# Heads of 22 float64 weight pieces: two ScalarE activations replaced by two GpSimd multiplications

## Chip, cores and metric

One core of a Trainium2 chip runs the whole program in one launch. The metric is the device time of that core in microseconds (us). The engines are TensorE (PE in the profile, its weight loads PEld), VectorE (DVE), ScalarE (ACT), GpSimd (POOL) and SyncE (SP), which issues most of the DMA transfers.

## The reference

Three stages follow one another. Attention with a top-32 mask over 4 x 8 heads gives 2304 token rows of 512. A routing step gives each token to one of 8 experts, greedily by falling logit and with at most 288 tokens each. Each expert is a two-layer network; what it gives goes through one more layer pair, whose weights w_in and w_out are float64.

```
scores = scale * q @ k.T ; keep the 32 largest of a row ; softmax ; x = attn @ v
for idx in argsort(-(x @ w_gate).flatten()):        # routing
    tok, e = idx // E, idx % E
    if assigned[tok] < 0 and counts[e] < cap: assigned[tok] = e; counts[e] += 1
for e in range(E):
    y[mask_e] = maximum(x[mask_e] @ w1[e], 0) @ w2[e]
h = y @ w_in
g = (a0 + a1*h + a2*h*h + a3*h**3) / (1 + |b0|*|h| + |b1|*h*h + 1e-6)
out = g @ w_out                                      # w_in, w_out: float64
```

## The kernel before

**The stages in time.** Attention fills the first 442 us of the profiled execution. The routing search follows up to about 553 us, then the gathers of the first experts' tokens are prepared. From about 568 to 624 us lies a stretch that is called the transition here: PE computes expert 0's two layers while ACT and DVE finish w_in and w_out. From 624 us on PE multiplies by w_in and w_out, expert after expert, to the end.

**The float64 pieces.** TensorE works on float16 here, so each float32 or float64 weight becomes a pair of float16 numbers, high and low. w_in and w_out are cut into 32 pieces of 128 x 512 numbers: pieces 0 to 15 are w_in, 16 to 31 w_out, in blocks of four. `fetch` lets SP load a raw piece into a slot (of `region`, `win`, `wout` or `nraw`; the slot's name stands in the rows). A piece then goes through these steps:

- The heads. They take the top 16 bits of each float64 number (sign, 11 bits of exponent, 4 of fraction) and make of them the top of a float32. For the pieces of `quick` (6 to 19 before) these are two ACT instructions into a `ring` tile, of which there are three: Abs (L373) and Relu (L377). `signed` (L395) puts the sign in, and `mantissa` (L408) the lower bits of the fraction; both are DVE instructions on halves of 256 columns. For the other pieces from 6 on, the heads are three ACT instructions (L383 Sign, L384 Abs, L385 Relu), and DVE does `mantissa` and `apply_sign` (L412) on 512 columns.
- ACT squares the piece and sums (`square`, L306). When a block of four is done, a few small DVE instructions make its scales s_in or s_out (L293 to L298).
- ACT writes the scaled high part (`high`, L436), DVE the low part (`low`, L440). The raw slot is then free, and `fetch` loads the next piece into it.

When all of w_out's scales stand, DVE takes their minimum (ev_m, L1363), PE turns it (L1356), and behind these in PE's order stand the norm (L2061) and the first products with w_in (ph, L1929 to L1931).

**What sets the order.** A planner (class Flow) is given every one of these instructions with its engine, a cost, a rank and what it waits for, and writes each engine's instruction list before the program runs. Each engine carries its list out in order, and an instruction that is not ready holds up all that stand behind it. POOL's list holds, in routing, the updates of the assignment (asel L1690, asg L1711), and in the transition the gathers xe of the experts' token rows (L1906).

The program's functions that the diff touches:

Of the kernel before, what the change touches and what calls it, by code (L numbers as in the profile page):

```python
# [9 lines left out]
BF16 = mybir.dt.bfloat16  # L10
# [174 lines left out]
def kernel(  # L185
# [163 lines left out]
    bias16 = wpool.tile([P, 1], F32, name="bias16")  # L349
    nc.vector.memset(bias16, -896.0 * 2.0**7)  # L350
    QS = int(6)
    QE = int(20)
    ring, ring_of, ring_users = [], {}, []

    def quick(n):
        return QS <= n < QE
# [10 lines left out]
    def heads(n):  # L367
        top = top_of(n)
        if quick(n):
            def size():  # L370
                ring.append(ring.pop(0))
                ring_of[n] = ring[-1]
                nc.scalar.activation(upper_of(n).bitcast(BF16), top.bitcast(BF16), AF.Abs)  # L373

            return [
                ("A", 0.52, size),
                ("A", 0.52, lambda: nc.scalar.activation(  # L377
                    upper_of(n), upper_of(n), AF.Relu, scale=2.0**3, bias=bias16
                )),
            ]  # L380
        top = top.bitcast(BF16)
        return [
            ("A", 0.52, lambda: nc.scalar.activation(sign(n), top, AF.Sign)),  # L383
            ("A", 0.52, lambda: nc.scalar.activation(top, top, AF.Abs)),  # L384
            ("A", 0.61, lambda: nc.scalar.activation(  # L385
                value(n).bitcast(U32), top.bitcast(U16), AF.Relu, scale=2.0**19, bias=bias8
            )),
        ]
# [3 lines left out]

    def signed(n, o):
        up = upper_of(n)[:, o]
        nc.vector.scalar_tensor_tensor(up, top_of(n)[:, o], 0x8000, up, op0=OP.bitwise_and, op1=OP.bitwise_or)  # L395

    def in_parts(cost, fn, deps, rank, late, hv=None):

# [20 lines left out]
    def add_block(i, n0, dst, s, inv, rows, rank, late, after):  # L419

        o = slice(4 * i, 4 * i + 4) if rows else slice(i, i + 1)
        sq = wpool.tile([P, 4], F32, name="nq", bufs=8)
        steps = []
        n2 = sq
        if not rows:
            n2 = wpool.tile([P, 1], F32, name="nq1", bufs=8)
            steps.append(("V", 0.07, lambda: nc.vector.tensor_reduce(n2, sq, axis=AX.X, op=OP.add)))
        steps += [("V", 0.07, f) for f in power_steps(s[:, o], inv[:, o], n2, 410)]

        def part(g):  # L430
            j = 4 * i + g if rows else i
            return j, [d[:, j, :] if rows else d[:, i, g * 512 : (g + 1) * 512] for d in dst]

        def high(g):
            j, (h, l) = part(g)
            nc.scalar.activation(h, value(n0 + g).bitcast(F32), AF.Copy, scale=s[:, j : j + 1])  # L436

        def low(g):
            j, (h, l) = part(g)
            nc.vector.scalar_tensor_tensor(  # L440
                l, value(n0 + g).bitcast(F32), s[:, j : j + 1], h, op0=OP.mult, op1=OP.subtract
            )
            fetch(raw_t.pop(n0 + g))

        norms = []
        for g in range(4):
            n = n0 + g
            t = [arrived[n]]
            if quick(n):
                first = flow.add("A", 0.52, lambda n=n: heads(n)[0][2](), t, rank + 0.5, late)  # L450
                t = flow.add("A", 0.52, lambda n=n: heads(n)[1][2](), [first], rank + 0.5, late)
                t = in_parts(0.6, lambda o, n=n: signed(n, o), [t], rank + 0.4, late)
                t = in_parts(0.6, lambda o, n=n: mantissa(n, o), t, rank + 0.3, late)
                take(first, ring_users, ZR, t)
            else:
                for k in range(3 if n >= 6 else 0):
                    t = [flow.add("A", (0.52, 0.52, 0.61)[k], lambda n=n, k=k: heads(n)[k][2](), t, rank + 0.5, late)]
                if n >= EV:
                    parts = 1 if n >= QE else HV
                    t = in_parts(0.6, lambda o, n=n: mantissa(n, o), t, rank + 0.4, late, parts)  # L460
                    t = in_parts(0.6, lambda o, n=n: apply_sign(n, o), t, rank + 0.3, late, parts)
            norms.append(
                flow.add("A", 0.61, lambda n=n, g=g: square(value(n).bitcast(F32), sq[:, g : g + 1]), t, rank + 0.2, late)
            )
        scaled = flow.chain(steps[:-1], norms, rank, late)
        lows, LOWS = [], after
        last = flow.chain(steps[-1:], [scaled], rank + 0.3, late)
        for g in range(4):
            t = flow.add("A", 0.61, lambda g=g: high(g), [scaled] + (lasts[-1] if lasts else []), rank + LOWS, late)
            t = flow.add("V", 0.66, lambda g=g: low(g), [t], rank + LOWS + 0.1, late)  # L470
            lows.append(t)
        lasts.append(lows)
        return last

    with ExitStack() as actx:
# [862 lines left out]
            for i in range(2):  # L1338
                fetch((arena2[:, i, 1024 * b : 1024 * (b + 1)], 4 * KC + 4 * b - 1, None))
        for i in range(ZR):  # L1340
            ring.append(lpool.tile([P, 512], U32, name=f"ring{i}", bufs=1))
            nc.gpsimd.memset(ring[-1], 0)
        NRAW = 4
        for i in range(NRAW):
            fetch((npool.tile([P, 1024], U32, name=f"nraw{i}", bufs=1), NP, None))

# [1047 lines left out]
```

## Time and profile before

| | before |
|---|---|
| median of three runs | 1222.1 us (1221.91 to 1222.24) |
| profiled execution | 1227.85 us, span 1226.1 us |
| PE busy | 1114.8 us (91%) |
| DVE busy | 1056.6 us (86%) |
| ACT busy | 1021.4 us (83%) |
| POOL busy | 381.4 us (31%), 487 instructions |
| granted TensorE clock, mean | 0.921 |

Shares are means over stages with different limits. The profiled execution is a run of its own beside the three; its span is the time from its first to its last recorded instruction. POOL's busy time lies almost all in attention.

### The profile page before, as it was taken

How to read it: one execution, taken by the hardware profiler on the slowest of the kernel's cores; microseconds unless marked ns; L12 is line 12 of the kernel's file. 1: busy time of each engine (PE TensorE's matmuls, PEld its weight loads, DVE VectorE, ACT ScalarE, POOL GpSimd, SP SyncE). 2: the span in 40 equal slices, each digit the busy share in tenths (PEclk: the TensorE clock that was granted, in tenths of full speed). 3: DMA queues.
4: the chain of work that ended last, by engine and by line, in shares of the span. 5: the costliest groups of instructions: out<-in, count | busy, mean ns of one | idle time of the engine just before them, and what ended most of it. 6: DMA issues, size and time to landing. Idle time of an engine off the chain costs nothing.

```text
span 1226.1 us, 26893 instructions
## 1 busy us (share of the span) xinstructions
PE 1114.8 (91%) x9719; PEld 900.6 (73%) x9719; DVE 1056.6 (86%) x4094; ACT 1021.4 (83%) x1810; POOL 381.4 (31%) x487
## 2 busy tenths in 40 slices
PE   4899999999999986884749999999999999999996
PEld 3688888888888854653536778888888888888784
DVE  6999999988989937886898879898989889897795
ACT  4899999999999847577989978888888788876684
POOL 4788888877778400002010001110101000001010
PEclk9899999999999975555978999999999999999998
DMA  5205202112000307411242222221112221000000
GB/s 125 51 10 162 50 13 51 36 34 51 2 2 1 138 2 285 148 53 58 104 151 76 69 89 89 89 88 70 56 54 89 89 78 68 33 2 20 1 21 20
DMA packets 81105, 80.59 MB, mean 66 GB/s; under 512 B 59968, under 2 KB 59968, under 8 KB 80960
## 3 DMA queue, kind: packets, MB, share of 16 engines
q1 hardware_dynamic: 77888, 69.27, 17.9%
q0 software_dynamic: 3072, 9.48, 2.6%
q8 instruction: 80, 1.31, 0.4%
q14 instruction: 65, 0.53, 0.1%
HBM read 69.25 MB, written 9.47 MB: 64 GB/s over the span
## 4 chain that ended last, share of the span: by engine, by line
PE 27%; issue 15%; ACT 6%; DVE 4%; POOL 1%; DMA 1%; POOLq 0%; DVEq 0%
PE pa L1929 3%; PE pa L1930 3%; PE ph L1929 3%; PE pa L1931 3%; PE ph L1930 3%; PE ph L1931 3%; PE po L1930 3%; PE po L1931 3%; PE po L1929 3%; ACT junk L306 2%; POOL out_dram L2315 1%; ACT w1s L1402 1%; PE pa L2304 0%; ACT wout L383 0%; DVE w2s L1407 0%
## 5 line engine op out<-in xcount | busy, mean ns | idle before, releaser
L785 POOL TENSOR_TENSOR win<-sv,sg 128x576 f32<-128x576 f32 x142 | 179.3, 1284 | 65.2 <-ACT sg L780 49.6
L749 DVE MAX8 cd<-sv 128x8 f32<-128x82 f32 (+1 forms) x1008 | 178.5, 231 | 12.0 <-ACT sv L702 11.9
L1929 PE MATMUL ph<-x,win 128*128 128x288 f16 x512 | 148.2, 289 | 11.2 <-DVE uv L2198 11.2
L883 PE MATMUL po<-vm,pT 128*128 128x65 f32 (+1 forms) x1280 | 151.3, 266 | 0.7 <-DVE x L903 0.4
L1930 PE MATMUL po<-g,wout 128*128 128x288 f16 x512 | 147.6, 288 | 2.2 <-DVE g L1920 2.1
L1929 PE MATMUL po<-g,wout 128*128 128x288 f16 x512 | 147.6, 288 | 0.9 <-ACT g L1919 0.8
L1930 PE MATMUL ph<-x,win 128*128 128x288 f16 x512 | 148.2, 289 | 0.0
L1931 PE MATMUL ph<-x,win 128*128 128x288 f16 x512 | 148.2, 289 | 0.0
L1931 PE MATMUL po<-g,wout 128*128 128x288 f16 x512 | 147.6, 288 | 0.0
L883 PEld LDWEIGHTS po<-vm,pT 128*128 128x128 f32 (+1 forms) x1280 | 139.3, 182 | 3.4 <-PE pt L855 1.1
L851 PE MATMUL pt<-ident,sv 128*128 128x128 f32 x648 | 126.3, 283 | 0.0
L2315 POOL DMA_INDIRECT out_dram<-ob,tok x24 | 25.5, 1063 | 317.5 <-ACT ob L2311 266.7
L855 PE MATMUL pt<-dg,mk 128*128 128x128 bf16 x720 | 120.5, 221 | 1.5 <-POOL mk L842 1.3
L1906 POOL DMA_INDIRECT xe<-xrows,rows_i x24 | 24.6, 1026 | 297.9 <-PE pa L1941 274.8
L780 ACT ACTIVATE sg<-sv,cut_all 128x576 bf16<-128x576 f32 x142 | 109.3, 779 | 4.9 <-DVE cut_all L755 4.9
L2189 ACT ACTIVATE z<-ph,inv 128x288 f32<-128x288 f32 x128 | 64.0, 500 | 59.0 <-PE ph L1931 58.4
L841 ACT ACTIVATE sg<-sv,pn 128x576 bf16<-128x576 f32 x136 | 98.2, 774 | 12.9 <-POOL pn L819 12.9
L692 PE MATMUL s<-region 64*128 64x288 f32 (+1 forms) x640 | 92.7, 438 | 16.2 <-ACT region L663 11.8
L786 DVE MAX8 w<-win 128x8 f32<-128x576 f32 x142 | 105.5, 744 | 0.0
L851 PEld LDWEIGHTS pt<-ident,sv 128*128 128x128 f32 x648 | 92.5, 143 | 16.2 <-issue 3.9
L842 POOL TENSOR_SCALAR mk<-sg 128x576 bf16<-128x576 bf16 x136 | 89.1, 674 | 1.8
L865 ACT ACTIVATE pT<-pt 128x1152 f32<-128x1152 f32 x72 | 81.4, 1131 | 4.8 <-PE pt L855 4.6
(359 smaller groups left out, 3315.7 us busy)
## 6 DMA issues: line engine op xcount, KB each, us to landing
region<-in_moe_w_dram SPq DMA_DIRECT2D x16, 2048.0 KB, 7.9
xrows<-x SPq DMA_DIRECT2D x1, 4644.0 KB
region<-in_q_dram SPq DMA_DIRECT2D x32, 128.0 KB, 2.8
region<-in_k_dram SPq DMA_DIRECT2D x32, 128.0 KB, 2.7
vm<-in_v_dram SPq DMA_DIRECT2D x32, 128.0 KB, 3.1
wout<-in_moe_w_in_dram SPq DMA_DIRECT2D x8, 511.8 KB, 6.8
region<-in_moe_w_out_dram SPq DMA_DIRECT2D x8, 511.8 KB, 3.4
win<-in_moe_w_in_dram SPq DMA_DIRECT2D x6, 511.8 KB, 7.8
```

Source lines behind the costliest of these rows:

```text
L692: nc.tensor.matmul(sc[p0 : p0 + n, 2 * hh + g, 0:w], qT[rows, j, p0 : p0 + n], kT[rows, bb, c : c + w], start=True, stop=True,)
L749: nc.vector.max(cd[:, g, :], sv[:, o : o + n])
L780: nc.scalar.activation(sg, sv_t[u, hh], AF.Sign, bias=cut_all[:, 2 * u + hh, 7:8], scale=-OVER, accum_out=t["sum"][:, c : c + 1],)
L785: nc.gpsimd.tensor_tensor(win, sv_t[u, hh], sg, op=OP.mult)
L786: later.append(lambda c=c, win=win: nc.vector.max(t["w8"][:, c, :], win))
L841: nc.scalar.activation(sg, sv, AF.Sign, bias=t["pn"][:, c : c + 1])
L851: nc.tensor.transpose(dst, pr[:, c * P : (c + 1) * P], ident)
L855: nc.tensor.matmul(dst, mk_buf[u % 2][:, o : o + P], bat[b]["dg"][:, 2 * i + hh, :], start=False, stop=True, skip_group_check=True,)
L883: nc.tensor.matmul(po[p0 : p0 + n, i, hh, :], sb[:, hh * (R + 1) + c, p0 : p0 + n], vm[:, bb, hh, c, :], start=(c == 0), stop=False,)
L1929: nc.tensor.matmul(acc, ah, bh, start=first, stop=False)
L1930: nc.tensor.matmul(acc, ah, bl, start=False, stop=False)
L1931: nc.tensor.matmul(acc, al, bh, start=False, stop=last)
```

## The change

Pieces 6 to 27 are now `quick`. Their heads are two POOL instructions: `narrow` multiplies the top 16 bits, read as bfloat16, by 2^-112 into the ring tile, and `widen` multiplies what came out, read as a 16-bit integer, by 8 into a 32-bit integer tile `wide`, of which there are two. `signed` takes the lower half of `wide` and the sign bit of the raw piece. From piece 20 on, `signed` and `mantissa` work on 512 columns. The raw `nraw` tiles are three instead of four. Lines below the edit stand 2 to 6 lines later (L395 is L397, L408 is L410, L412 is L414, L436 is L438, L440 is L442, L1356 is L1362, L1690 is L1696, L1711 is L1717, L1906 is L1912, L1941 is L1947).

```
-    QE = int(20)
+    QE = NP - 4
     ring, ring_of, ring_users = [], {}, []
+    wide, wide_of, wide_users = [], {}, []
...
     def heads(n):
         top = top_of(n)
         if quick(n):
-            def size():
+            def narrow():
                 ring.append(ring.pop(0))
                 ring_of[n] = ring[-1]
-                nc.scalar.activation(upper_of(n).bitcast(BF16), top.bitcast(BF16), AF.Abs)
-
-            return [
-                ("A", 0.52, size),
-                ("A", 0.52, lambda: nc.scalar.activation(
-                    upper_of(n), upper_of(n), AF.Relu, scale=2.0**3, bias=bias16
-                )),
-            ]
+                nc.gpsimd.tensor_scalar(upper_of(n).bitcast(BF16), top.bitcast(BF16), 2.0**-112, None, op0=OP.mult)
+
+            def widen():
+                wide.append(wide.pop(0))
+                wide_of[n] = wide[-1]
+                nc.gpsimd.tensor_scalar(wide_of[n], upper_of(n), 8.0, None, op0=OP.mult)
+
+            return [("G", 0.7, narrow), ("G", 0.7, widen)]
...
     def signed(n, o):
         up = upper_of(n)[:, o]
-        nc.vector.scalar_tensor_tensor(up, top_of(n)[:, o], 0x8000, up, op0=OP.bitwise_and, op1=OP.bitwise_or)
+        mag = wide_of[n].bitcast(U16).rearrange("p (n w) -> p n w", w=2)[:, o, 0]
+        nc.vector.scalar_tensor_tensor(up, top_of(n)[:, o], 0x8000, mag, op0=OP.bitwise_and, op1=OP.bitwise_or)
...
-                first = flow.add("A", 0.52, lambda n=n: heads(n)[0][2](), t, rank + 0.5, late)
-                t = flow.add("A", 0.52, lambda n=n: heads(n)[1][2](), [first], rank + 0.5, late)
-                t = in_parts(0.6, lambda o, n=n: signed(n, o), [t], rank + 0.4, late)
-                t = in_parts(0.6, lambda o, n=n: mantissa(n, o), t, rank + 0.3, late)
+                first = flow.add("G", 0.7, lambda n=n: heads(n)[0][2](), t, rank + 0.5, late)
+                second = flow.add("G", 0.7, lambda n=n: heads(n)[1][2](), [first], rank + 0.5, late)
+                parts = 1 if n >= 20 else HV
+                t = in_parts(0.66, lambda o, n=n: signed(n, o), [second], rank + 0.4, late, parts)
+                take(second, wide_users, 2, t)
+                t = in_parts(0.66, lambda o, n=n: mantissa(n, o), t, rank + 0.3, late, parts)
                 take(first, ring_users, ZR, t)
...
-            ring.append(lpool.tile([P, 512], U32, name=f"ring{i}", bufs=1))
+            ring.append(npool.tile([P, 512], U32, name=f"ring{i}", bufs=1))
             nc.gpsimd.memset(ring[-1], 0)
-        NRAW = 4
+        for i in range(2):
+            wide.append(npool.tile([P, 512], U32, name=f"wide{i}", bufs=1))
+        NRAW = 3
```

The planner writes other lists for this. In routing, POOL's list before holds nothing but the updates of the assignment:

```order
L1690 TENSOR_TENSOR asg<-oh,gone 128x144
L1690 TENSOR_TENSOR asel<-oh,gone 128x144
L1711 TENSOR_TENSOR asg<-asg,asel 128x144
L1690 TENSOR_TENSOR asel<-oh,gone 128x144
L1711 TENSOR_TENSOR asg<-asg,asel 128x144
```

Now narrow (L374) and widen (L379) stand between them, one to five in each gap but the last:

```order
L1696 TENSOR_TENSOR asel<-oh,gone 128x144
L1717 TENSOR_TENSOR asg<-asg,asel 128x144
L379 TENSOR_SCALAR wide_12933<-ring_12931 128x512
L1696 TENSOR_TENSOR asel<-oh,gone 128x144
L1717 TENSOR_TENSOR asg<-asg,asel 128x144
L374 TENSOR_SCALAR ring_12927<-wout 128x512
L379 TENSOR_SCALAR wide_12934<-ring_12927 128x512
L374 TENSOR_SCALAR ring_12929<-wout 128x512
L379 TENSOR_SCALAR wide_12933<-ring_12929 128x512
L1696 TENSOR_TENSOR asel<-oh,gone 128x144
L1717 TENSOR_TENSOR asg<-asg,asel 128x144
```

An update now stands behind whatever heads the planner put ahead of it. Routing has 11 narrows and 10 widens in all. The other 23 of the 44 stand after routing, in the transition, among the gathers xe, which were twelve in a row before:

```order
L1912 DMA xe<-xrows,rows_i 96x516 x3
L379 TENSOR_SCALAR wide_12933<-ring_12929 128x512
L374 TENSOR_SCALAR ring_12931<-region 128x512
L374 TENSOR_SCALAR ring_12927<-region 128x512
L379 TENSOR_SCALAR wide_12934<-ring_12931 128x512
L1912 DMA xe<-xrows,rows_i 96x516 x3
L379 TENSOR_SCALAR wide_12933<-ring_12927 128x512
L374 TENSOR_SCALAR ring_12929<-region 128x512
```

The three gathers of expert 0 come first, then four heads, the three of expert 1, nineteen heads more, and only then the six of experts 2 and 3.

On ACT, in the same stretch, heads of w_out pieces stood between expert 0's hidden activations (hT) and squares (junk) before:

```order
L306 ACTIVATE junk,nq<-nraw_12939 128x512
L1915 ACTIVATE hT_17254<-pe 128x288
L373 ACTIVATE ring_12927<-wout 128x512
L373 ACTIVATE ring_12929<-wout 128x512
L1915 ACTIVATE hT_17254<-pe 128x288
L377 ACTIVATE ring_12927<-ring_12927,bias_115 128x512
L377 ACTIVATE ring_12929<-ring_12929,bias_115 128x512
L1915 ACTIVATE hT_17254<-pe 128x288
L383 ACTIVATE wout<-wout 128x512 x2
L384 ACTIVATE wout<-wout 128x512 x2
L385 ACTIVATE wout<-wout,bias_111 128x512
```

Now none stands there, and expert 1's xT comes earlier in the list:

```order
L306 ACTIVATE junk,nq<-region 128x512
L1921 ACTIVATE hT_17240<-pe 128x288
L306 ACTIVATE junk,nq<-region 128x512
L1921 ACTIVATE hT_17240<-pe 128x288 x2
L306 ACTIVATE junk,nq<-wout 128x512
L1925 ACTIVATE xT_17431<-pa,s_x 128x288
L306 ACTIVATE junk,nq<-region 128x512
L1925 ACTIVATE xT_17431<-pa,s_x 128x288
```

DVE's list up to ev_m keeps its counts but for one kind: eight full `apply_sign` are now eight full `signed`. The twelve head instructions of pieces 28 to 31 stay on ACT, and stand in routing. On PE the last six transposes of expert 1's tokens (L1941), which stood in a row behind expert 0's last product and just ahead of ev_m's turn, now stand as two threes among expert 0's products of the second layer.

## Rows read from the trace of the kernel before

**Rows 1.** Windows: start:end, us; busy us (count) by engine; PEclk, DMA share, GB/s.

```profile
478.00:550.00 72.00, 62.53 (x695) 42.65 (x693) 61.58 (x294) 52.17 (x97) 4.44 (x10) 0.50 0.43 152
568.60:623.60 55.00, 30.80 (x219) 23.25 (x219) 50.83 (x128) 49.35 (x96) 8.43 (x9) 0.75 0.28 89
663.00:1226.00 563.00, 545.74 (x4469) 437.46 (x4467) 484.41 (x1043) 449.19 (x829) 42.67 (x63) 0.99 0.18 60
```

**Rows 2.** The chain that ended last, around 624 us: start, us, what.

```profile
622.24 0.76 ACT junk L306 x2
624.03 0.37 PE pa L1356
625.36 0.24 PE ph L1929
```

**Rows 3.** Waits, 568.6 to 663 us: us in total, times, longest.

```profile
PE pa L1941 <- DVE xT L1920: 12.2, 2, 12.0
PE pa L1356 <- DVE ev_m L1363: 8.2, 2, 5.8
```

**Rows 4.** Groups by line, ACT, 568.6 to 623.6 us.

```profile
L384 ACT ACTIVATE wout<-wout 128x512 bf16<-128x512 bf16 x4 | 5.3, 1388 | 0.0
L383 ACT ACTIVATE wout<-wout 128x512 int8<-128x512 bf16 x4 | 5.2, 1371 | 0.0
L385 ACT ACTIVATE wout<-wout,bias 128x512 uint32<-128x512 uint16 x4 | 3.0, 758 | 0.0
L377 ACT ACTIVATE ring<-ring,bias 128x512 uint16<-128x512 uint16 x3 | 2.5, 866 | 0.0
L373 ACT ACTIVATE ring<-wout 128x512 bf16<-128x512 bf16 x2 | 1.4, 768 | 0.0
L373 ACT ACTIVATE ring<-nraw 128x512 bf16<-128x512 bf16 x1 | 0.8, 779 | 0.0
```

**Rows 5.** Groups by line, DVE, same stretch: two with idle time before them.

```profile
L408 DVE SCALAR_TENSOR_TENSOR wout<-wout 128x512 uint32<-128x512 uint32 x4 | 2.8, 692 | 2.1 <-ACT wout L385 2.1
L1920 DVE SCALAR_TENSOR_TENSOR x<-pe,r_in,x 128x288 f16<-128x288 f32 x4 | 2.1, 516 | 1.2 <-ACT x L1919 1.2
```

**Rows 6.** Windows of one line each: L440, L408, L412, L395 on DVE.

```profile
568.60:623.60 55.00, 17.08 (x24) 0.75 0.28 89
...
568.60:623.60 55.00, 12.80 (x24) 0.75 0.28 89
...
568.60:623.60 55.00, 8.12 (x12) 0.75 0.28 89
...
568.60:623.60 55.00, 4.39 (x11) 0.75 0.28 89
```

**Rows 7.** Timeline in routing: start, us, engine, line, what.

```profile
477.01 0.18 DVE L1674 TENSOR_TENSOR vt<-top,pen 128x18 f32<-128x18 f32 x1
...
489.80 0.46 POOL L1711 TENSOR_TENSOR asg<-asg,asel 128x144 bf16<-128x144 bf16 x1
489.87 0.42 DVE L1674 TENSOR_TENSOR vt<-top,pen 128x18 f32<-128x18 f32 x1
```

**Rows 8.** Line L903 over the whole span: ns min/median/max, starts, forms.

```profile
L903 DVE TENSOR_TENSOR x<-po,den x28: 291/556/558, 61.0 to 441.5; 128x384 f32<-128x384 f32 x22, 128x128 f32<-128x128 f32 x6
```

**Rows 9.** The page's costliest groups: two of POOL's in attention.

```profile
L785 POOL TENSOR_TENSOR win<-sv,sg 128x576 f32<-128x576 f32 x142 | 179.3, 1284 | 65.2 <-ACT sg L780 49.6
...
L842 POOL TENSOR_SCALAR mk<-sg 128x576 bf16<-128x576 bf16 x136 | 89.1, 674 | 1.8
```

**Rows 10.** Timeline of POOL in routing, one round of the search.

```profile
513.42 0.43 POOL L1690 TENSOR_TENSOR asel<-oh,gone 128x144 bf16<-128x144 bf16 x1 [11.04 <-DVE rng L1563]
...
525.55 0.43 POOL L1690 TENSOR_TENSOR asel<-oh,gone 128x144 bf16<-128x144 bf16 x1 [11.17 <-DVE rng L1563]
```

**Rows 11.** Groups by line, DVE, 478 to 550 us.

```profile
L1599 DVE TENSOR_SCALAR_CACHE_REDUCE over<-pl 32x8 bf16<-32x8 f32 x24 | 3.8, 158 | 5.8 <-PE pl L1535 5.8
...
L427 DVE TENSOR_REDUCE nq<-nq 128x1 f32<-128x4 f32 x3 | 0.5, 154 | 1.6 <-ACT junk L306 1.6
```

## The prediction

> **What bounds the kernel now.** I first read the windows, stage by stage, to see which engine has no room left. From 663 us to the end it is PE: 545.74 of 563 us busy at a granted clock of 0.99 [rows 1]. The change puts nothing there, so whatever it does ahead of that stretch moves the end by the same time. In the transition PE is busy for only 30.80 of 55 us, DVE for 50.83 and ACT for 49.35 [rows 1]. Two engines are near full together there, and the reader should keep both in mind: taking work from one leaves the other.
>
> Next the chain around the end of the transition. It comes out of ACT's squares at 622.24 us, goes through DVE's small scale instructions to ev_m, then PE's turn at 624.03 and the first product with w_in at 625.36 [rows 2]. The waits say the same: PE stood still for 5.8 us before that turn, for ev_m [rows 3]. So what sets the start of the long PE stretch is when the last w_out scale stands, and that is a matter of ACT and DVE.
>
> In routing no engine is full: in the 72 us window PE is busy for 62.53 us, DVE for 61.58 and ACT for 52.17, POOL for 4.44 [rows 1]. The search runs in rounds; one takes 12.13 us from asel to asel, of which POOL idles 11.17 [rows 10]. DVE is the engine that every round passes through, with its list in order, and the preparation of pieces lies between the steps of the search.
>
> **What is taken from ACT.** In the transition the heads that leave ACT are 5.3 + 5.2 + 3.0 + 2.5 + 1.4 + 0.8 = 18.2 us [rows 4]. That is a third of the window, but it can't all come back: DVE itself works 50.83 of the 55 us. What DVE waits for there, and ACT ends, is 2.1 us (`mantissa` behind the head L385) and 1.2 us (x behind ACT's L1919) [rows 5]. Those 3.3 us are the most that this can give. I take them whole, **−3.3 us** (bounds 0 and −3.3), because 18.2 us of relief is far more than the wait. In routing DVE waits for ACT 1.6 us, for the squares ahead of nq [rows 11]; the heads there stand ahead of the squares in ACT's list and go too, so **−1.6 us** (bounds 0 and −1.6).
>
> DVE's own work changes little: eight full `signed` for eight full `apply_sign`, both with two tiles of 512 columns as input; the halves of L395 take 4.39 us for 11, and 8.12 us for 12 is the full L412 [rows 6], so a full `signed` costs at most 2 x 0.40 = 0.80 against 0.68, at most 1 us for eight. Two halves pay the fixed part of an instruction twice, so I put this at 0 and leave the 1 us to the range.
>
> **What POOL's work costs.** POOL has room: 44 instructions on an engine that idles nearly all of both stretches. The price of one is not shown, since before has no such operation with these strides. The nearest row is L842, one input, a multiplication's form, bfloat16 on 576 columns in 674 ns [rows 9]; 512/576 of it is 0.60 us. The upper bound is the two-input L785, 1284 ns on 576 columns [rows 9], or 1.14 us for 512. I take 0.60, as the form is L842's.
>
> POOL's time in itself is hidden. What matters is what a POOL instruction does to DVE. L1674 on DVE, a small instruction with two inputs in SBUF, takes 0.18 us when POOL is idle. At 489.87 us it takes 0.42, when POOL's L1711 runs since 489.80 for 0.46 us; it ends as L1711 ends, at about 490.28 [rows 7]. So a two-input DVE instruction was held until POOL was done. L903, where one of the two inputs is PSUM, has a median of 556 ns and a longest of 558 for the wide form [rows 8], although POOL is busy beside most of attention. The hold is thus on DVE instructions with both inputs in SBUF.
>
> The Trainium skill (SBUF — State Buffer, "Who interferes with whom") states it so: a DVE instruction with two SBUF inputs and a GpSimd instruction that reads SBUF exclude each other for a whole instruction, whichever began first. By this rule all 44 heads hold DVE, one input or two. The trace agrees as far as it goes, 0.42 against 0.18 us; no row shows a one-input POOL instruction against a two-input DVE one.
>
> How much of DVE's list is of that kind? In the transition L440, L408, L412 and L395 are 17.08 + 12.80 + 8.12 + 4.39 = 42.4 us of 50.83 busy [rows 1, 6], a share of 0.83 by time; by count 71 of 128, 0.55. A POOL instruction that starts when DVE ends one holds the next if that is of the kind, and part of the one after it if not. I take 0.7, between the two: 0.7 x 0.60 = 0.42 us a head, and this is nearest to how DVE's mixture alternates.
>
> In the transition 23 heads give 23 x 0.42 = **+9.7 us** (bounds 0, if there is no hold, and 23 x 0.60 = 13.8). DVE is full there once ACT no longer holds it up, so nothing covers this. In routing 21 heads give 21 x 0.42 = 8.8 us. DVE waits 5.8 us in all for PE's counts (L1599) [rows 11], and a piece's instruction held in such a wait costs nothing. I let that cover a third: **+5.9 us** (bounds 0 and 21 x 0.60 = 12.6).
>
> The Trainium skill (GPSIMD Engine Reference, § 3.1) gives about 1.8 cycles an element at best and 769 ns for 512 elements. With that estimate the two terms would be 12.4 and 7.5 us and the time 1237. L842 is below this figure with its 674 ns for 576 elements, so the row decides here.
>
> **What else moves.** Expert 1's gathers stand behind four heads, and nineteen heads behind these gathers, which wait for PE's transposes of expert 0. That is early, ahead of expert 0's products, and only the pieces of w_out wait for it: 0. The six transposes that moved ahead on PE let PE wait within expert 0's products instead of behind them, where it now waits 12.0 us for xT [rows 3]. As PE has 5.8 us to spare before ev_m's turn [rows 3], I cost this at 0; without that cover it would cost what exceeds 5.8 us. Three raw tiles instead of four make piece 17 arrive in the transition; it stands late in DVE's list: 0.
>
> **The sum.** −3.3 − 1.6 + 9.7 + 5.9 = +10.7 us. On the profiled execution's 1227.85 us (span 1226.1) that is 1238.6; the median of the runs is 5.75 us below that execution, so the forecast is 1222.1 + 10.7 = 1232.8, or 1233 us.
>
> **The rivals.**
>
> *A one-input POOL instruction does not hold DVE: faster.* All holds I saw are by instructions with two inputs (L1711 in rows 7). If one input leaves DVE alone, both positive terms are gone and what is left is −3.3 − 1.6 = −4.9 us: 1217 us. For it: no row of before contradicts it. Against it: a one-input POOL instruction still has to read SBUF, and the hold followed DVE's second input, as L903 shows. It decides for faster when a head's hold falls below 4.9/37 = 0.13 us (37 being 23 heads and two thirds of 21). Chance 0.22.
>
> *The holds fall into waits: no change.* If routing's all lie in the 5.8 us of L1599's waits, and the transition's are cut to half because DVE reaches the end of its two-input instructions just as POOL does, it is 4.9 − 4.9 = 0, so 1222 us, give or take 2. For it: routing has slack on each engine. Against it: the transition has none on DVE. Chance 0.09.
>
> *POOL's instructions are slow with these strides: much slower.* The heads read two bytes out of eight and write two of four. At 1.14 us instead of 0.60 the holds are 15.6 x 1.9 = 29.6 us, which gives 1222.1 + 24.7 = 1247 us; then POOL's pairs also make `signed` late. For it: no row has such strides. Against it: POOL's price in L842 is for the same form. Chance 0.09.
>
> **How the numbers follow.** The forecast, with 0.60, goes from 1227 (share 0.55, and two thirds of routing's holds covered: 7.6 + 2.3 − 4.9 = +5.0) to 1239 (share 0.83, nothing covered: 11.5 + 10.5 − 4.9 = +17.1). The range takes in the faster rival at its lower end and part of the slow one: 1217 to 1241. The change must exceed 0.2%, 2.4 us, to be told from none. Faster 0.22, within 0.09, slower 0.60 + 0.09 = 0.69.
>
> **What would show it.** In the changed profile: L374 and L379 near 0.60 us each; `signed`, `mantissa` and `low` longer where they lie beside a head, ending some tens of ns behind it, and L1916 (one input in PSUM) not; L1527 the same in routing, with rounds longer than 12.13 us; ev_m's turn in the transition later by about 6 us counted from the stretch's start; ACT with idle time; the stretch behind ev_m as long as now. Unchanged durations beside the heads would prove the first rival; heads near 1.1 us the last. I am also wrong if PE reaches ev_m's turn late on account of the moved transposes, or if asel behind a waiting head lengthens the rounds by more than the holds do.

## The result, and the profile after

The change makes the kernel slower: the ratio to before is 1.0134, with an interval from 1.0114 to 1.0153. On the 1222.1 us of before that is 1238.5 us (1236.0 to 1240.8), or 16.4 us more. The median of four runs was 1241.2 us, beside 1222.17 for the kernel before in the same comparison. Runs of the kernel before spread from 1222 to 1230 us in the comparisons below, so whole times are compared by ratio here, and stretches by their traces. The profiled execution has a span of 1239.5 us, 13.4 more than before; that is less than the 16.4 of the ratio, and the execution profiled before was, with 1227.85 us, one of the longer ones of its kernel.

The windows of the changed kernel, for the stages of [rows 1] (the transition is longer now, and the last stage starts later):

```profile
core 0: us, PE busy (x) PEld busy (x) DVE busy (x) ACT busy (x) POOL busy (x), PEclk, DMA share, GB/s
478.00:550.00 72.00, 62.86 (x696) 43.00 (x694) 67.50 (x294) 27.17 (x64) 36.86 (x31) 0.50 0.42 147
568.60:638.40 69.80, 31.57 (x219) 23.02 (x219) 56.09 (x127) 35.20 (x78) 52.66 (x32) 0.74 0.25 79
677.00:1239.00 562.00, 545.54 (x4468) 437.37 (x4466) 485.42 (x1045) 449.32 (x831) 42.12 (x63) 0.99 0.18 60
```

The last stage is as it was, 545.54 us of PE's work against 545.74 [rows 1]. Routing takes as long as before, although DVE is busy there for 67.50 us instead of 61.58. The transition has grown from 55 to 69.8 us. In it ACT has become idle half of the time (35.20 of 69.8), DVE too has room (56.09 of 69.8), and POOL is busy for 52.66, where it was 8.43. PE's longest wait for ev_m shows the loss in one line:

```profile
PE pa L1362 <- DVE ev_m L1369: 28.0, 2, 24.8
```

It was 5.8 us [rows 3]. What DVE waits for in the transition, by its groups (the middle column is busy us and mean ns, the last the idle time and its cause):

```profile
L397 DVE SCALAR_TENSOR_TENSOR ring<-wout,wide 128x256 uint16<-128x256 uint16 (+1 forms) x9 | 5.1, 588 | 5.5 <-POOL wide L379 5.5
L397 DVE SCALAR_TENSOR_TENSOR ring<-region,wide 128x512 uint16<-128x512 uint16 x4 | 2.9, 728 | 4.9 <-POOL wide L379 4.9
L397 DVE SCALAR_TENSOR_TENSOR ring<-nraw,wide 128x256 uint16<-128x256 uint16 (+1 forms) x5 | 2.4, 494 | 1.4 <-POOL wide L379 1.4
L1944 DVE CAST tok<-xe 96x3 int32<-96x3 f32 x2 | 0.4, 188 | 1.9 <-DMA xe<-xrows,rows_i 1.9
```

`signed` waits 5.5 + 4.9 + 1.4 = 11.8 us for `widen`; the waits for ACT of [rows 5] are gone. And the heads themselves, on POOL in the same stretch:

```profile
L379 POOL TENSOR_SCALAR wide<-ring 128x512 uint32<-128x512 uint16 x12 | 19.9, 1655 | 3.5 <-DVE tok L1944 2.6
L374 POOL TENSOR_SCALAR ring<-wout 128x512 bf16<-128x512 bf16 x6 | 11.7, 1961 | 2.2 <-DVE region L410 1.9
...
L374 POOL TENSOR_SCALAR ring<-region 128x512 bf16<-128x512 bf16 x4 | 8.4, 2109 | 0.2
L374 POOL TENSOR_SCALAR ring<-nraw 128x512 bf16<-128x512 bf16 x1 | 2.2, 2185 | 0.1
```

A head takes 1.66 to 2.19 us, by the means of these groups, where the prediction has 0.60. Twenty-three of them are 42.2 us in a stretch of 69.8, in one queue. The chain that ended last goes through that queue (start, us, what):

```profile
613.97 2.17 POOL ring L374
...
617.80 2.17 POOL ring L374
...
621.62 2.19 POOL ring L374
623.89 1.51 POOL wide L379
625.42 0.73 DVE ring L397
626.15 1.96 DVE wout L442 x3
...
638.65 0.37 PE pa L1362
```

The reader is to see that DVE's `signed` (L397) and the low parts (L442) only start when POOL's last head is done. ev_m's turn is at 638.65 us, against 624.03 [rows 2]: 14.6 us later, while the first gather of the stretch starts at 567.59 against 567.51.

The holds that the prediction speaks of are there as well. The timeline shows one on L442, a two-input instruction that takes 0.74 us when no head runs beside it (the first row):

```profile
591.45 0.74 DVE L442 SCALAR_TENSOR_TENSOR win<-wout,s_in,win 128x512 f16<-128x512 f32 x1
...
593.24 2.04 POOL L374 TENSOR_SCALAR ring<-wout 128x512 bf16<-128x512 bf16 x1 [1.87 <-DVE region L410]
593.68 1.13 DVE L442 SCALAR_TENSOR_TENSOR win<-wout,s_in,win 128x512 f16<-128x512 f32 x1
```

The second one, of 1.13 us, ends at 594.81, 0.47 us before the head does, so it was not held to the head's end. Added up over all DVE instructions beside a head (the time above the median of the same line and shape without one) the holds are 5.7 us in the transition, 0.25 for each of the 23 heads, and 7.5 us in routing, 0.36 for each of the 21.

In routing they cost nothing. DVE's idle time in the 72 us window fell from 72 − 61.58 = 10.42 us to 72 − 67.50 = 4.50; its waits for PE's counts went from 5.8 us [rows 11] to

```profile
L1605 DVE TENSOR_SCALAR_CACHE_REDUCE over<-pl 32x8 bf16<-32x8 f32 x24 | 3.7, 156 | 2.4 <-PE pl L1541 2.1
```

and the wait for ACT ahead of nq, 1.6 us there, to 0.0. Some rounds are longer than the 12.13 us of [rows 10]: this one takes 13.05 us, and POOL reaches asel without idle time, just done with a head:

```profile
513.81 0.43 POOL L1696 TENSOR_TENSOR asel<-oh,gone 128x144 bf16<-128x144 bf16 x1 [0.18 <-DVE rng L1569]
...
526.86 0.47 POOL L1696 TENSOR_TENSOR asel<-oh,gone 128x144 bf16<-128x144 bf16 x1
```

But the last asel of routing starts at 553.15 us, against 553.27 before.

So there were three candidates for the loss: heads that come late because POOL takes so long (theory 1), the holds (theory 2), and what else the change moves, with one raw tile less (theory 3).

### The profile page after: what moved, and what is told of

It reads as the page before. It is cut to its first block, busy times and chain, and to the rows that moved or that the text cites. A ratio compares the mean times of both kernels' runs of the same rounds, so it can differ in the third digit from the quotient of the medians.

```text
span 1239.5 us, 26942 instructions
## 1 busy us (share of the span) xinstructions
PE 1113.7 (90%) x9719; PEld 900.0 (73%) x9719; DVE 1068.3 (86%) x4094; ACT 978.9 (79%) x1758; POOL 458.9 (37%) x531
## 4 chain that ended last, share of the span: by engine, by line
PE 26%; issue 15%; DVE 5%; POOL 3%; ACT 3%; DMA 1%; POOLq 0%; DVEq 0%; SPq 0%
PE pa L1935 3%; PE pa L1936 3%; PE pa L1937 3%; PE ph L1935 3%; PE ph L1937 3%; PE ph L1936 3%; PE po L1936 3%; PE po L1937 3%; PE po L1935 3%; POOL ring L374 1%; ACT junk L306 1%; POOL wide L379 1%; POOL out_dram L2321 1%; ACT w1s L1408 1%; DVE wout L442 1%
## 5 line engine op out<-in xcount | busy, mean ns | idle before, releaser
L1935 PE MATMUL ph<-x,win 128*128 128x288 f16 x512 | 148.3, 290 | 11.3 <-DVE uv L2204 11.3
L1912 POOL DMA_INDIRECT xe<-xrows,rows_i x24 | 26.6, 1110 | 261.5 <-PE pa L1947 242.0
```

The lines of the kernel that those rows point to most:

```text
L1935: nc.tensor.matmul(acc, ah, bh, start=first, stop=False)
```

## The experiments

The measure that carries most of what follows is the time from the start of the first gather (the first L1906 or its successor, where routing is over) to the end of the span. It leaves out what lies ahead: the first update of the assignment (L1690 or its successor) starts anywhere between 471 and 478 us in these traces, although the kernels hardly differ up to there. The ratio is that of the runs, with its interval.

Two cautions on this measure. It is one execution of each kernel, and a difference of a few microseconds in it isn't clear: behind ev_m's turn PE was busy for 571.66 to 578.10 us with the same 4647 matrix products, from trace to trace. And the planner writes its lists anew for nearly every kernel. Only the kernel with two operations has, on all engines, the lists of the change, instruction by instruction; the one with idle heads in the transition has those of the kernel with heads on ACT, apart from what it adds on POOL.

| kernel | first gather, us | span, us | difference | ratio to before |
|---|---|---|---|---|
| before | 567.5 | 1226.1 | 658.6 | |
| the change | 567.6 | 1239.5 | 671.9 | 1.0134 (1.0114 to 1.0153) |
| heads on ACT | 563.8 | 1223.8 | 660.0 | 1.0005 (0.9983 to 1.0027) |
| GpSimd heads, pieces 6 to 16 | 566.7 | 1225.9 | 659.2 | 1.0021 (1.0001 to 1.0041) |
| GpSimd heads, pieces 17 to 27 | 564.6 | 1234.5 | 669.9 | 1.0102 (1.0070 to 1.0135) |
| two operations in a head | 562.5 | 1223.6 | 661.1 | 1.0028 (1.0012 to 1.0045) |
| planner's cost 1.6 | 568.6 | 1231.7 | 663.1 | 1.0070 (1.0050 to 1.0090) |
| idle heads, both stretches | 577.5 | 1238.2 | 660.7 | 1.0102 (1.0072 to 1.0132) |
| idle heads, transition | 566.7 | 1229.3 | 662.6 | 1.0019 (1.0002 to 1.0037) |
| no heads | 561.5 | 1215.8 | 654.3 | 0.9950 (0.9932 to 0.9967) |
| two operations, planner's cost 0.9 | 567.0 | 1228.9 | 661.9 | 1.0031 (1.0014 to 1.0049) |
| heads shared by ACT and GpSimd | 566.8 | 1225.2 | 658.4 | 1.0000 (0.9986 to 1.0014) |

### Heads on ACT

The heads go back to ACT, all else of the change stays: 22 quick pieces, three raw tiles, wide `signed` and `mantissa` from piece 20 on.

```
+    def on_pool(n):
+        return False
...
+        if quick(n) and not on_pool(n):
...
+                nc.scalar.activation(upper_of(n).bitcast(BF16), top.bitcast(BF16), AF.Abs)
...
+                    upper_of(n), upper_of(n), AF.Relu, scale=2.0**3, bias=bias16
```

> All that the change does stays (22 quick pieces, three raw tiles, wider signed and mantissa from piece 20 on), but the heads are made by ACT, with the two activations that the kernel before has for its quick pieces. Theory 1, late heads (a head takes GpSimd 1.5 to 2.2 us instead of 0.60, and in the transition the pieces wait for GpSimd): the loss is gone, 1217 to 1223 us. Theory 2, holds (VectorE is lengthened beside each head, and that is the cost): the same. Theory 3, slots and order (one raw tile less, transposes moved ahead in TensorE's list): the loss stays, 1235 us or more.

The time is that of before (1.0005), and 660.0 us from the first gather on. Theory 3 is out: neither the missing raw tile nor the wider instructions cost the 13 us. The result also has a point that none of the theories had: pieces 20 to 27 now cost ACT two activations instead of three, yet nothing is gained. ev_m does stand earlier, 51.3 us behind the first gather instead of 56.2. Part of it is given back just behind, as PE's waits after 610 us show:

```profile
PE pa L1379 <- DVE ev_m L1386: 13.7, 1, 13.7
PE ph L1952 <- DVE uv L2221: 9.2, 5, 3.5
PE pa L1383 <- DVE ev_g L1388: 2.4, 1, 2.4
```

ev_g, the step behind ev_m, comes 2.4 us late for PE; DVE's low parts stand ahead of it. The windows from ev_m's turn to the end of the span, of before and of this kernel, give the rest:

```profile
624.03:1226.13 602.10, 575.80 (x4647) 458.06 (x4647) 517.37 (x1120) 484.78 (x891) 42.67 (x63) 0.98 0.19 63
615.45:1223.82 608.37, 578.10 (x4647) 458.94 (x4647) 520.77 (x1124) 486.02 (x895) 41.97 (x63) 0.97 0.19 62
```

With heads on ACT this stretch is 6.3 us longer. PE idles 4.0 us more in it and is busy 2.3 us more with as many products, at a granted clock of 0.97 instead of 0.98; DVE has four instructions more to do there. So ev_m's turn alone does not set the end.

### GpSimd heads in one stretch only

Two kernels from the one above: pieces 6 to 16 get GpSimd heads, 20 of the 22 in routing, or pieces 17 to 27, 17 of the 22 in the transition.

```
+    def on_pool(n):
+        return n <= 16        # in the other kernel: n >= 17
```

> GpSimd heads for pieces 6 to 16 only, which lie in routing but for one; ACT's two activations for 17 to 27. Theory 1: as with all heads on ACT, within 2 us, since routing has room for late heads and for holds. Theory 2: the holds of routing, 6 to 8 us by what VectorE's busy time grew there, come on top of the kernel with all heads on ACT.

> GpSimd heads for pieces 17 to 27 only, which lie in the transition; ACT's two activations for 6 to 16. Theory 1: nearly the whole loss, 1235 to 1241 us, the turn of ev_m 10 us or more later than with all heads on ACT. Theory 2: 5 to 6 us more than with all heads on ACT.

The first costs nothing that can be told from all heads on ACT (1.0021 and 1.0005, with overlapping intervals; 659.2 and 660.0 us from the first gather on), the second 11.3 of the 13.3 us that the change costs from the first gather on. The loss belongs to the transition. There DVE waits for `widen` as in the change, though for 5.6 us only, and the rest of this kernel's loss I did not follow:

```profile
L412 DVE SCALAR_TENSOR_TENSOR ring<-wout,wide 128x256 uint16<-128x256 uint16 (+1 forms) x9 | 5.1, 584 | 4.2 <-POOL wide L394 4.2
L412 DVE SCALAR_TENSOR_TENSOR ring<-region,wide 128x512 uint16<-128x512 uint16 x4 | 2.8, 731 | 1.4 <-POOL wide L394 1.4
```

### The price of a multiplication on GpSimd

The kernel before, with rows of GpSimd multiplications on 512 columns of scratch added behind its last output. First alone, three of each form, then with two-input DVE instructions beside them.

```
+    def narrow_form():
+        ops(by4, by8, 0.5, None, op0=OP.mult)
+
+    def widen_form():
+        ops(wid.bitcast(U32), by4.bitcast(U16), 8.0, None, op0=OP.mult)
+
+    def dense_form():
+        ops(w16[:, 0:512], r16[:, 0:512], 0.5, None, op0=OP.mult)
```

> The kernel before with a row of GpSimd multiplications on 512 columns added behind its last output, alone first and then beside two-input VectorE instructions; only their durations are read. Theory 1: narrow and widen 1.5 us or more when alone, and the same with dense operands about 0.60 (if it is the strides) or as long as these (if it is the operation). Theory 2: about 0.60 alone, and 1.5 only beside VectorE.

The timeline, three of narrow, widen, dense bfloat16 and dense float32 alone (start, us of all three):

```profile
1220.25 5.18 POOL L2375 TENSOR_SCALAR region<-region 128x512 bf16<-128x512 bf16 x3
1225.51 4.64 POOL L2378 TENSOR_SCALAR region<-region 128x512 uint32<-128x512 uint16 x3
1230.23 4.63 POOL L2381 TENSOR_SCALAR region<-region 128x512 bf16<-128x512 bf16 x3
...
1258.62 4.64 POOL L2400 TENSOR_SCALAR region<-region 128x512 f32<-128x512 f32 x3
```

One takes 1.5 us, with dense operands as with strided ones and whatever the type; only narrow's strides add 0.2. So the rival of the prediction that named the strides had the wrong reason, and theory 2 is wrong in that it wanted DVE to be what makes a head long. L842, my nearest row, took 674 ns on 576 columns [rows 9]. What it has and the heads have not is a second operation: it multiplies and adds. The next kernel puts that to the test.

```
+        ops(by4, by8, 0.5, 0.0, op0=OP.mult, op1=OP.add)
...
+        ops(wid.bitcast(U32), by4.bitcast(U16), 8.0, 0.0, op0=OP.mult, op1=OP.add)
...
+        ops(w16[:, 0:512], r16[:, 0:512], 0.5, 0.0, op0=OP.mult, op1=OP.add)
...
+        ops(w16[:, 0:512], r16[:, 0:512], 0.5, None, op0=OP.mult)
```

> The kernel before with GpSimd multiplications on 512 columns added behind its last output; only their durations are read. So far a multiplication by one constant took 1.49 us alone on 512 columns, with dense operands as with strided ones, where L842, a multiplication and an addition in one instruction, took 0.67 us on 576. Theory 1a, the form: with a second operation (an addition of 0 or a multiplication by 1) the same columns take about 0.60 us. Theory 1b, the place: they take 1.5 us as well, and L842's price belongs to something else in attention.

The same columns with a second operation (L2374 narrow, L2378 widen, L2382 dense), then dense with one (L2386), and dense on 256 columns with one (L2390) and with two (L2392):

```profile
1219.55 2.47 POOL L2374 TENSOR_SCALAR region<-region 128x512 bf16<-128x512 bf16 x3
...
1224.63 2.03 POOL L2378 TENSOR_SCALAR region<-region 128x512 uint32<-128x512 uint16 x3
...
1228.85 2.03 POOL L2382 TENSOR_SCALAR region<-region 128x512 bf16<-128x512 bf16 x3
...
1233.06 4.66 POOL L2386 TENSOR_SCALAR region<-region 128x512 bf16<-128x512 bf16 x3
...
1242.53 2.72 POOL L2390 TENSOR_SCALAR region<-region 128x256 bf16<-128x256 bf16 x3
1245.33 1.39 POOL L2392 TENSOR_SCALAR region<-region 128x256 bf16<-128x256 bf16 x3
```

With an addition of 0 behind the multiplication an instruction takes 0.62 us instead of 1.5, and narrow 0.76. A multiplication by 1 in place of the addition gave the same durations, and an addition alone, without a multiplication, 1.49 us. By the columns it is (4.66 − 2.72) / 3 / 256 = 2.5 ns a column with one operation, and (2.03 − 1.39) / 3 / 256 = 0.83 ns with two. It is the form.

The first of these kernels shows the hold by itself too. Its DVE instructions beside POOL's, ns min/median/max:

```profile
L2412 DVE SCALAR_TENSOR_TENSOR region<-region x36: 691/693/1003, 1266.2 to 1295.1; 128x512 f32<-128x512 f32 x36
```

Beside a 1.5 us multiplication every second of them took 0.98 to 1.00 us instead of 0.69, the one between ran through undisturbed; beside a memset on POOL none was longer. So one multiplication holds one instruction, for 0.29 to 0.31 us, and not for its own length. Beside the two-operation forms of the second kernel each DVE instruction took 1.07 (narrow) or 0.98 us (widen), a hold of 0.38 or 0.29:

```profile
L2400 DVE SCALAR_TENSOR_TENSOR region<-region x30: 691/693/1074, 1248.1 to 1272.8; 128x512 f32<-128x512 f32 x30
```

### Two operations in each head

```
-                nc.gpsimd.tensor_scalar(upper_of(n).bitcast(BF16), top.bitcast(BF16), 2.0**-112, None, op0=OP.mult)
+                nc.gpsimd.tensor_scalar(upper_of(n).bitcast(BF16), top.bitcast(BF16), 2.0**-112, 0.0, op0=OP.mult, op1=OP.add)
...
-                nc.gpsimd.tensor_scalar(wide_of[n], upper_of(n), 8.0, None, op0=OP.mult)
+                nc.gpsimd.tensor_scalar(wide_of[n], upper_of(n), 8.0, 0.0, op0=OP.mult, op1=OP.add)
```

> The change with narrow and widen as they are, but each with a second operation, the addition of 0. Theory 1a: the heads take about 0.6 to 0.8 us, GpSimd is no longer late, and the time falls to 1222 to 1230 us. Theory 1b: no difference to the change, 1240 us. Theory 2 (holds of VectorE are the cost): 1235 us or more, as there are as many heads.

The addition of 0 takes away 10.8 of the 13.3 us (671.9 to 661.1), and the ratio falls from 1.0134 to 1.0028. In the transition a widen takes 0.88 us and a narrow 0.80 to 1.12, and DVE never waits for one:

```profile
L379 POOL TENSOR_SCALAR wide<-ring 128x512 uint32<-128x512 uint16 x12 | 10.6, 882 | 6.8 <-DVE tok L1944 4.5 <-DVE ring L397 1.0 <-DVE pw_v L294 0.7
...
L397 DVE SCALAR_TENSOR_TENSOR ring<-wout,wide 128x256 uint16<-128x256 uint16 (+1 forms) x9 | 5.0, 590 | 0.0
L397 DVE SCALAR_TENSOR_TENSOR ring<-region,wide 128x512 uint16<-128x512 uint16 x4 | 3.3, 850 | 0.0
```

The holds did not go with the lateness: added up as above they are 6.4 us in this transition, 0.28 a head. The number of heads is the same, and so is every engine's list, instruction by instruction, so nothing but the length of the heads differs: this is the closest test of theory 1 against theory 2.

### The planner's cost

```
-            return [("G", 0.7, narrow), ("G", 0.7, widen)]
+            return [("G", 1.6, narrow), ("G", 1.6, widen)]
...
-                first = flow.add("G", 0.7, lambda n=n: heads(n)[0][2](), t, rank + 0.5, late)
+                first = flow.add("G", 1.6, lambda n=n: heads(n)[0][2](), t, rank + 0.5, late)
```

> The change, with the planner's cost of a head at 1.6 instead of 0.7. Theory 1: the lists can take GpSimd's real pace into account, so that VectorE does other work in between: 1230 to 1238 us, but not the time before. Rival (the planner's wrong cost is all there is to it): 1222 us.

1.0070, about half of the loss. From the first gather on it is 663.1 us, and so 8.8 of the 13.3 are gone there, although the heads are as slow as in the change. With the real pace in the planner, DVE's waits for `widen` in the transition are 3.5 + 1.4 = 4.9 us instead of 11.8:

```profile
L397 DVE SCALAR_TENSOR_TENSOR ring<-wout,wide 128x256 uint16<-128x256 uint16 (+1 forms) x9 | 5.8, 680 | 3.5 <-POOL wide L379 3.5
...
L397 DVE SCALAR_TENSOR_TENSOR ring<-region,wide 128x512 uint16<-128x512 uint16 x4 | 2.9, 728 | 1.4 <-POOL wide L379 1.4
```

So slow heads cost as much as they do only together with lists made for 0.7 us a head. Such lists are half of the loss by the ratios and two thirds by the traces; the rest stays.

### Idle heads

Heads on ACT again, and multiplications on GpSimd that nobody waits for, to have the holds alone. The first try gave two to the planner for each piece.

```
+                for _ in range(2):
+                    flow.add("G", 0.7, lambda: nc.gpsimd.tensor_scalar(wide[1], wide[0], 8.0, None, op0=OP.mult), [arrived[n]], rank + 0.5, late)
```

> Heads of pieces 6 to 27 on ACT, the rest as in the change; for each of these pieces GpSimd does two multiplications of a zero tile when the piece has arrived, and nobody waits for them. What is left is the holds. Theory 1: 0 to 5 us more than with all heads on ACT. Theory 2: the loss of the change, 13 us or more.

It came out as theory 2 has it, 1.0102, but for a reason of its own. The planner put eleven in a row, and POOL's update asel stood behind them:

```profile
474.73 17.96 POOL L473 TENSOR_SCALAR wide<-wide 128x512 uint32<-128x512 uint32 x11
492.77 0.43 POOL L1714 TENSOR_TENSOR asel<-oh,gone 128x144 bf16<-128x144 bf16 x1
```

A round that takes 12 us took 18.5. The whole loss is in routing: the first gather came at 577.5 us, and from there the kernel took 660.7, as with all heads on ACT (660.0). This run says nothing on holds; it shows what late updates of the assignment cost. The second try puts 23 multiplications in a row behind the gathers of expert 1, where no update waits:

```
+        for _ in range(23 if e == 1 else 0):
+            nc.gpsimd.tensor_scalar(wide[1], wide[0], 8.0, None, op0=OP.mult)
```

> All heads on ACT, as in the first experiment, and in the transition, behind the gathers of expert 1, 23 GpSimd multiplications of a zero tile in a row, 1.5 us each, for which nobody waits and which no assignment update stands behind. Only the holds of VectorE are left. Theory 1 (late heads are the cost): the stretch from the first gather to ev_m grows by 0 to 6 us over the 51.3 us with all heads on ACT, far from the 70.7 of the change. Theory 2 (holds): it grows by 15 us or more.

They ran through the transition from end to end:

```profile
578.17 43.96 POOL L1935 TENSOR_SCALAR wide<-wide 128x512 uint32<-128x512 uint32 x23
```

The holds add up to 6.8 us, 0.30 for each. From the first gather to ev_m the time grew from 51.3 to 56.3 us, and to the end from 660.0 to 662.6. So holds alone, as many as the change has, cost 2.6 us of 13.3 in these traces. By the ratios, 1.0019 and 1.0005 with overlapping intervals, they can't be told from nothing, and they are far from the whole loss.

### No heads

The heads of pieces 6 to 27 are left out; `signed` takes its bits from a constant.

```
-        mag = wide_of[n].bitcast(U16).rearrange("p (n w) -> p n w", w=2)[:, o, 0]
+        mag = wide[0].bitcast(U16).rearrange("p (n w) -> p n w", w=2)[:, o, 0]
...
-                first = flow.add("G", 0.7, lambda n=n: heads(n)[0][2](), t, rank + 0.5, late)
-                second = flow.add("G", 0.7, lambda n=n: heads(n)[1][2](), [first], rank + 0.5, late)
```

> The heads of pieces 6 to 27 are left out, on every engine: signed joins the sign bit to a constant, so that the numbers of these pieces are not the weights. VectorE does what it does in the change, ACT and GpSimd have nothing to do for the heads. This is the whole relief of ACT with nothing paid for it. By the prediction's terms for ACT: 4.9 us less than before, 1217 to 1219 us. Rival (the relief is given back behind ev_m, as with all heads on ACT): within 2.4 us of before.

0.9950 (0.9932 to 0.9967), which on 1222.1 us is 6.1 us less (4.0 to 8.3); 654.3 us from the first gather on, 4.3 less than before. This is what leaving out every head is worth, with lists made for it, when nothing is paid. It does not come about as the prediction has it, by an earlier ev_m. The turn of ev_m stands at 622.43 us, 60.9 us behind the first gather, where before had 56.5. But the planner has put the first 48 products with w_in ahead of that turn, where before had none:

```profile
604.83 0.45 PE L1939 MATMUL ph<-x,win 128*128 128x288 f16 x1
...
622.43 0.27 PE L1366 MATMUL pa<-ident,ev_m 128*1 128x128 f32 x1
```

What PE does earlier it need not do later: from the turn to the end it takes 593.4 us instead of 602.1. How much of the gain is ACT's relief and how much the other order on PE, no run separates.

### Other versions

Two attempts at a version that beats both kernels: two operations with the planner's cost at 0.9, and two operations for the odd pieces with ACT's activations for the even ones.

```
-            return [("G", 0.7, narrow), ("G", 0.7, widen)]
+            return [("G", 0.9, narrow), ("G", 0.9, widen)]
```

> The change with two operations in each head (0.6 to 0.8 us) and the planner's cost of a head at 0.9 instead of 0.7, which is nearer to what the heads took beside VectorE. Theory 1: 1222 to 1228 us, not faster than before by what can be told, as the holds (6 to 8 us in the transition) eat the relief. Rival (heads at this price pay): 1219 us or less.

```
+    def on_pool(n):
+        return n % 2 == 1
```

> The heads of pieces 6 to 27 shared out: GpSimd with two operations for the odd pieces, ACT's two activations for the even ones, else as the change. With all heads on ACT the time was that of before, without any heads 6 us less, with all of them on GpSimd at this price 3 us more. Theory: half the holds (3 to 4 us in the transition) against half of what ACT is relieved of, 1219 to 1226 us, no gain that can be told. Rival (the two engines together have the room): 1218 us or less.

1.0031 and 1.0000. The first is like its sister with 0.7. The second is the kernel before in time, with half of the heads on each engine. No version with heads was faster than before.

## Why the prediction came out as it did

The direction and the range were right: 1238.5 us by the ratio, in 1217 to 1241 (the median of the four runs, 1241.2, lies at its very end). The terms were not. By the table, from the first gather on the change costs 13.3 us where the prediction has −3.3 + 9.7 = +6.4, and ahead of it nothing (the first gather starts at 567.59 against 567.51) where it has −1.6 + 5.9 = +4.3.

That the total came out in the range is luck: late heads, 10.8 us by the runs, were left out, and the holds were put too high by 7.1 us in the transition (2.6 instead of 9.7) and by 5.9 in routing.

**What bounds the kernel.** Right for the change. From ev_m's turn to the end of the span it is 1239.5 − 638.65 = 600.9 us, against 1226.1 − 624.03 = 602.1. What the transition loses, the end loses. It is no rule for other lists: that stretch is 608.4 us with heads on ACT and 593.4 without heads, so an earlier or later ev_m is not by itself a faster or slower kernel.

**The price of a head: the first step that failed.** I took 0.60 us from L842 "as the form is L842's". The form is not: L842 has a second operation, and that is a factor of 2.4 on 512 columns (1.5 against 0.62 us, both measured alone). The chosen row had the operation's name and the engine, but not the operands of the instruction. Even the upper bound of 1.14 us was below the measured 1.5.

**Late heads: the second step that failed, priced at nothing and the largest term.** The prediction says "POOL's time in itself is hidden". It mentions under the slow rival that "POOL's pairs also make `signed` late", and has no number for it. At 23 heads of 1.83 us (42.2 us by the rows above), in lists made for 0.7 us each, POOL's queue sets the pace: DVE waits 11.8 us for `widen`, and ev_m's turn comes 14.6 us later, where the prediction named 6 as the sign. That this is the cause is shown by the kernel with two operations, which has as many heads in the same lists and takes 10.8 us less; that the lists have a part in it is shown by the planner's cost of 1.6. I gave the slow rival a chance of 0.09 and 1247 us; its direction was right, its mechanism (longer holds) and its reason (strides) were not.

**The holds.** They exist for one-input heads, which was the open point of the faster rival: that rival is out. But each is 0.25 us in the transition and 0.36 in routing instead of 0.42, since a head of 1.5 us holds DVE for a part of itself only. The Trainium skill (SBUF — State Buffer, "Who interferes with whom") calls the ports that the two share an exclusive lock, and says, where it speaks of DVE's two-port mode, that whoever issues first has them for the whole instruction. The prediction took the whole instruction for two-input DVE instructions too. For these the measurement differs: 0.29 to 0.31 us of 1.5. The same section says that a GpSimd instruction that only writes SBUF does not contend with a two-input DVE one, and with that the trace agrees: six memsets of 0.53 us lengthened none. In time, 23 holds alone cost 2.6 us where the prediction has 9.7. From no heads to cheap ones on GpSimd it is 661.1 − 654.3 = 6.8 us; the holds, 6.4 us of DVE's time there, are the only part of this that I measured apart, and the lists differ as well.

**Routing.** Holds of 7.5 us were foreseen as 8.8, and the covered part as a third. All of it was covered: DVE had 10.4 us idle in the window, the waits for PE's counts and for ACT among them, and 5.9 of it was filled.

**The relief of ACT.** −4.9 us was forecast, and no heads at all gave −6.1 (−8.3 to −4.0). The size fits; the way is not shown. The prediction has DVE's waits for ACT vanish and ev_m come earlier, but without heads ev_m's turn comes 4.4 us later from the first gather on, and the gain goes with products that PE does ahead of it. With heads on ACT, where a part of the relief is left and the turn does come earlier, nothing was gained. So the fit of this term is luck as far as the runs tell.

**What I had put at 0** (raw tiles, moved transposes, wider instructions) stayed small: with heads on ACT and all of that in place the time is that of before. In the change PE waits 24.8 us in front of ev_m's turn, so the moved transposes never set the end.

From the first gather on, the rows of the table go from before to no heads by −4.3 us, from there to cheap heads on GpSimd by +6.8, and from these to slow ones by +10.8, together +13.3. Only the last step compares equal lists, so only it has a single cause shown.

## What to carry to other kernels

Take the price of an instruction from a row with the same number of operations and the same kind of operands, not only the same name; where no such row exists, a row of them on scratch behind the last output gives it in one run. When work moves to an idle engine, count what that engine's queue then takes in the stretch that is bound, and who waits at its end: 23 x 1.8 us in a stretch of 55 us left little room, however idle the engine was over the whole span, and in lists made for 0.7 us a head DVE waited 11.8 us. And a hold that falls into another engine's idle time is free, as routing's were; the same instructions cost most where two engines are full.

## What the runs showed of the hardware

On GpSimd a multiplication by one constant, with no second operation, took 1.49 us on 512 columns and 0.85 on 256; with an addition of 0 behind it 0.62 and 0.41, and with a multiplication by 1 on 512 columns 0.62 too. Narrow's strides added 0.14 to 0.21 us; the types that I tried changed nothing that can be told. The Trainium skill (GPSIMD Engine Reference, § 3.1) gives 769 ns for 512 elements as measured best; the runs show 0.62 for one form, below that, and 1.49 for another. Why one operation is the slower I could not tell.

A GpSimd multiplication held a two-input DVE instruction for 0.29 to 0.38 us, the short form longer (0.38 for the strided narrow, 0.29 for widen) than the slow one (0.31 and 0.29); what the long form does in the rest of its 1.5 us does not keep DVE off. A head can be lengthened too: behind the last output widen took 1.49 us alone and 1.66 where it began in the middle of a DVE instruction, and narrow's groups in the transition average 1.96 to 2.19 us, against 1.65 to 1.70 alone.
